# An H3 head and an S5 head on one core: row pairs of k, v, q and the output as two half transfers by parity, the filter's quarter matmuls for kv, and C's tiles transposed on TensorE

## The chip, the cores and the metric

The kernel runs on one core of one Trainium2 chip. The metric is the device time of one execution in microseconds, the median of several runs. All times here are of that core.

## The reference, cut to what matters

Two heads work side by side on sequences of S = 2048 steps and D = 1024 channels, and their outputs are put next to each other, bf16, [1, 2048, 2048]:

```python
def _A_ref(q, k, v, shift_k, ssm_k, ssm_D):
    for t in range(ks):                                   # ks = 4 taps
        k_shift = k_shift + k_pad[:, t:t + S, :] * shift_k[:, ks - 1 - t][None, None, :]
    kv = k_shift * v
    # a causal convolution over time, per channel, by transforms of length 2 * S = 4096
    y_f = rfft(pad(kv)) * rfft(pad(ssm_k))
    y = irfft(y_f)[:S] + kv * ssm_D
    return q * y
def _B_ref(x, Lambda_re, Lambda_im, B_re, B_im, C_re, C_im, log_dt, Dskip):
    Bu = jnp.einsum("bld,pd->blp", x, B_bar)              # B_bar, Lam_bar complex
    for t in range(L):
        h = Lam_bar[None, :] * h + Bu[:, t, :]
    return 2.0 * jnp.einsum("blp,dp->bld", hseq, Cmat).real + x * Dskip
return jnp.concatenate([a, b], axis=-1)
```

## The kernel before, in words

**Head B** goes through time in 16 chunks i of 128 steps. `x.i` loads a chunk transposed (a transposing DMA, L449). `U.i.jp.b` multiplies it by B, 16 matmuls of 128x128 (L468); `ue` copies the result from PSUM (ACT, L473). On DVE `r1` (L486), `r2` (L493) rotate it, `sc` scans (L499, two per chunk), `r3` (L486), `r4` (L505) rotate back; `cy` (ACT, L495) carries the last state over. `y.i.dh.part` (chunks 0 to 2, 14, 15; L515, L518) or `yq.i.k` (64x64 quarters of the array, chunks 3 to 13; L533) multiplies by C and adds the skip; `ye` evicts (L551). B is loaded in 16 tiles (`bl`), each transposed by 8 matmuls with the identity (`bT`, L417) and copied to BT (`bc`, ACT L433; one tile `bcv` on DVE, L431). Of C's 16 tiles eight come that way (`cl` L437, `cT` L417, `cc` ACT L441) and eight by a transposing DMA straight into CT (`cx`, L439). rtab, the scan's table of factors, is filled by ACT (`rta`, L379).

**Head A** does its transforms as matmuls. Time is split as t = 16 m + s: row m of 128 lies on partition m, and s = 0 to 15 counts steps. `kp.r` loads the row pair s = 2r, 2r + 1 of k (512 KB on 128 partitions) into a ring of 8 rows, `vp.r` of v, `qp.r` of q, all from SP's queue (L565 to L568, L573, L741). For each s `kvm`, `kva`, `kvb` (L582/584, L589, L595) make the 4-tap sum on DVE and `kvc` (L597) multiplies by v. `am.s.dh` (L602) is the first transform stage: two full 128x128 matmuls of 512 columns, one for each parity p of m, with F1t, whose rows of the other parity are zero. `ae` evicts (ACT, L608), `ast` stores to Ys_kv (POOL's queue, L611). The filter goes the same way in its own layout: `hl`, `hT` (transposes, L626), `hc` (ACT copy, L631), `hm` (L651), `he` (ACT, L659), `hst` (POOL's queue, L662). `hm` uses the quarter form: two row halves of the array by two column halves, FQt, four matmuls of 64x64 by 512 columns. The second stage works on 32 groups: `lw` loads the weights (L666, three slots), `lh`/`lk` the spectra (L671), `sh`/`sk` transform (quarters, L682), `she`/`ske` evict (L691, L698), `sw`/`swp` swap odd and even partitions by DMA (L702), `pr` multiplies (DVE, L708), `sa` transforms back (quarters, L720), `sae` evicts, `vst` stores Vs. The last stage: `vl` loads, `a3.s.dh` (L748) accumulates two full matmuls with Gt, one per parity, into one bank; `a3e` evicts, `qm` multiplies by q (DVE, L757), `ost`/`osp` store a row pair (POOL's or SP's queue, L758/759).

**What sets the order.** ORDER is a table of some 1500 words written into the kernel, run under a manual schedule: each task's instructions go to their engine's list in the table's order, and every engine runs its list in order. Letters after a colon give the slots: `a` a unit of the arena in SBUF (53 units of 2 KB per partition), `p` a PSUM bank of eight, `h` and `w` slots for states and weights. A task that reuses a slot waits for the slot's last reader. A suffix `v` puts an eviction on DVE. SP and POOL issue DMAs from their queues, each in order too, so a DMA behind one that waits is late as well.

Of the kernel before, what the change touches and what calls it, by code (L numbers as in the profile page):

```python
# [32 lines left out]
def a_constants():  # L33
# [37 lines left out]
bc.0.1 bc.7.0 bl.0.0:a46 tabA1:a24a51a14a12 kp.-1 bT.1.1:p2 x.0:a47 par_rest cl.0.0:a39 wb.1:p7 bT.5.0:p5 sin1
bl.3.0:a31 bcv.4.0 bT.0.0:p3 wbe.1 bT.4.1:p6 bc.1.1 tabA2 kring bl.3.1:a46 kvm.3:a26 gz bT.6.1:p1 bc.0.0 bl.1.0:a23
bc.4.1 U.0.2.0:a34p4 U.0.0.0:p2 sin2 bc.6.1 bl.2.1:a22 bT.3.1:p0 bc.5.0 x.1:a33 eo kvm.2:a18 kvm.1:a40 U.0.2.1
bT.1.0:p5 kva.2 cT.0.0:p1 bT.2.1:p3 bc.2.1 bT.3.0:p6 kva.1 kvb.2:a38 kva.3 bc.3.0 U.1.2.0:a36p7 stt U.1.2.1 bl.6.0:a50
bT.6.0:p3 kvb.1:a46 bl.7.1:a32 bc.3.1 U.0.1.0:p6 bT.7.1:p0 kp.-2 bc.1.0 bc.6.0 bc.7.1 U.0.1.1 U.0.0.1 ue.0.0 ue.0.1
vp.1:a48 cl.2.0:a22 z2 z1 cl.1.1:a31 cc.0.0 x.3:a21 cl.2.1:a44 ue.1.2 ue.0.2 U.0.3.0:p3 U.0.3.1 kvb.3:a32 ue.0.3
U.1.3.0:p6 U.1.0.0:p2 kvm.0:a13 cT.2.0:p0 U.1.3.1 U.1.1.0:p5 kvc.3 kvc.2 kva.0 r1.0:a48 cc.2.0 lw.1:w0 cl.1.0:a30
ue.1.3 cx.5.1 U.1.0.1 ue.1.0 cT.1.0:p3 cc.1.0 cl.3.0:a45 kvb.0:a39 am.2.1:p4p0 ae.2.1.1:a28 rta r2.0:h0 am.2.0:p6p2
cT.2.1:p1 cc.2.1 U.1.1.1 ue.1.1 cT.3.0:p3 vp.0:a42 kvc.1 U.3.2.0:a34p7 cc.3.0 ae.2.0.1 kvc.0 ae.2.0.0 kp.3 sc.0.1
U.3.2.1 hl.0.1:a24 cl.3.1:a20 cT.3.1:p0 sc.0.0 cc.3.1 am.3.0:p5p1 ae.3.1.0:a22 ae.2.1.0 r1.1:a42 hl.0.0 U.3.3.0:p3  # L80
U.3.3.1 cT.1.1:p0 cc.1.1 kp.2 hl.1.0:a48 cl.0.1:a38 ue.3.2 am.3.1:p4p1 ae.3.1.1 U.3.0.0:p6 ue.3.3 U.3.0.1 ue.3.0
ae.3.0.0 hl.1.1 am.1.1:p0p2 ae.1.1.1:a30 cx.5.0 am.0.0:p1p7 ae.0.1.0:a18 ae.3.0.1 r3.0:a12 hdv.1 ast.2 hdv.0 ast.3
U.3.1.0:p3 r4.0 ae.0.0.0 U.3.1.1 x.2:a52 cT.0.1:p5 am.1.0:p6p4 hT.0.4:p7 r2.1:h1 ae.1.0.1 am.0.1:p0p1 hT.0.7:p2
ae.1.1.0 hc.0.4:a16 hT.0.3:p4 ae.1.0.0 hT.0.0:p7 kvm.6:a12 ue.3.1 hT.0.6:p6 hc.0.3:a17 ae.0.0.1 cy.1 cc.0.1 ld_Q
hc.0.0:a46 ae.0.1.1 U.2.1.0:a44p3 r1.3:a40 U.2.1.1 ast.1 sc.1.1 U.2.2.0:p4 hc.0.7:a23 U.2.2.1 U.2.0.0:p5 ast.0 lw.0:w1
cx.6.0 cx.6.1 ue.2.2 U.2.0.1 cx.4.1 ue.2.1 hc.0.6:a20 ue.2.0 r2.3:h2 hT.0.1:p3 hT.0.2:p7 hc.0.1:a22 sc.1.0
hm.0.6.1:p1p2 hm.0.6.0:p4p6 he.0.6.0.0:a34 U.2.3.0:p0 hT.0.5:p3 hc.0.2:a41 U.2.3.1 hm.0.3.0:p5p4 he.0.6.1.1 he.0.6.1.0
he.0.3.0.0:a42 cx.7.0 kvm.5:a36 he.0.6.0.1 y.0.0.0:p7 kva.6 hc.0.5:a40 hm.0.7.1:p1p5 hm.0.3.1:p2p6 he.0.3.1.1 y.0.0.1
kvm.4:a24 he.0.3.1.0 he.0.7.1.1:a30 y.0.0.2 he.0.3.0.1 cx.4.0 cx.7.1 ue.2.3 he.0.7.1.0 y.0.0.3 hm.0.4.0:p2p6
ye.0.0:a17 hm.0.5.1:p5p4 hm.0.5.0:p0p3 he.0.4.0.0:a48 hst.0.6.1 he.0.5.0.0:a18 hst.0.6.0 he.0.5.1.0 he.0.5.0.1  # L90
y.0.1.0:p1 y.0.1.1 kvb.6:a20 he.0.5.1.1 kva.4 hm.0.4.1:p2p7 hm.0.7.0:p5p0 he.0.4.0.1 he.0.7.0.0 he.0.7.0.1 y.0.1.2
y.0.1.3 he.0.4.1.0 r3.1:a12 he.0.4.1.1 kvb.4:a23 hm.0.2.1:p6p4 he.0.2.1.0:a34 hst.0.3.1 x.4:a32 ye.0.1 he.0.2.1.1 r4.1
hm.0.0.1:p5p0 he.0.0.1.1:a50 U.4.1.0:a24p2 U.4.1.1 hm.0.2.0:p7p6 hm.0.0.0:p3p4 kva.5 he.0.2.0.1 hst.0.3.0 he.0.2.0.0
r1.2:a12 he.0.0.1.0 he.0.0.0.1 y.1.0.0:p1 hst.0.5.0 y.1.0.1 hst.0.5.1 kvb.5:a16 ue.4.1 hm.0.1.1:p7p5 hst.0.4.1
hm.0.1.0:p0p6 he.0.1.1.1:a38 he.0.1.0.1 y.1.0.2 vp.2:a28 hst.0.4.0 he.0.1.0.0 y.1.0.3 kvc.4 r2.2:h0 cy.2 he.0.0.0.0
ye.1.0:a18 kvc.5 am.5.1:p5p6 am.5.0:p4p2 am.4.1:p0p1 y.1.1.0:p3 y.1.1.1 he.0.1.1.0 hst.0.0.0 ae.5.1.1:a36 ae.4.0.1:a28
ae.5.1.0 hst.0.0.1 kp.5 am.4.0:p7p6 y.1.1.2 ae.4.1.0 vp.3:a26 ae.5.0.1 y.1.1.3 hl.3.0:a40 ae.5.0.0 hl.3.1 hd.3
ae.4.0.0 kvm.7:a12 hst.0.1.0 hl.2.0:a44 sc.2.1 kvc.6 hl.2.1 hd.2 am.6.0:p4p2 kva.7 ae.6.0.0:a22 ae.4.1.1 ast.5 sc.2.0
U.4.3.0:p6 ye.1.1 ae.6.1.0 kvb.7:a19 U.4.3.1 r3.2:a48 ue.4.3 am.6.1:p0p5 hT.1.1:p4 ae.6.0.1 kp.4 hc.1.1:a33 hT.1.3:p3
hc.1.3:a16 hst.0.1.1 ae.6.1.1 U.4.2.0:p2 hT.1.7:p0 U.4.2.1 yst.1 hc.1.7:a20 ue.4.2 ast.4 hT.1.6:p7 hc.1.6:a38  # L100
kvm.8:a12 U.4.0.0:p4 kvc.7 U.4.0.1 ue.4.0 r4.2 hT.1.0:p6 kva.8 ast.6 hc.1.0:a39 am.7.1:p0p2 am.7.0:p7p1 ae.7.1.0:a28
hT.1.4:p3 yst.0 hst.0.7.0 hc.1.4:a18 hst.0.2.0 ae.7.1.1 kvm.9:a48 y.2.0.0:p4 x.6:a37 ae.7.0.0 hm.1.3.1:p5p6 kvb.8:a36
he.1.3.1.1:a26 y.2.0.1 he.1.3.1.0 y.2.0.2 ae.7.0.1 cy.3 hm.1.7.1:p7p1 hm.1.3.0:p6p5 he.1.7.1.0:a16 hm.1.7.0:p3p0
he.1.3.0.1 he.1.3.0.0 he.1.7.0.1 he.1.7.0.0 kva.9 y.2.0.3 ye.2.0:a19 sc.3.1 vp.4:a22 y.2.1.0:p7 hT.1.2:p2 sc.3.0
hm.1.4.1:p0p6 hm.1.4.0:p3p5 kvc.8 hT.1.5:p4 r3.3:a44 y.2.1.1 ast.7 kvb.9:a18 y.2.1.2 hst.0.7.1 hst.1.3.1 he.1.7.1.1
y.2.1.3 he.1.4.1.0:a12 he.1.4.1.1 hst.1.3.0 hc.1.5:a20 he.1.4.0.1 he.1.4.0.0 am.8.1:p5p6 r4.3 ye.2.1 hst.1.4.1
ae.8.1.1:a40 am.8.0:p0p4 U.6.1.0:a14p1 hc.1.2:a52 U.6.1.1 ae.8.1.0 x.5:a36 ae.8.0.0 hst.0.2.1 ue.6.1 r1.4:a48 ae.8.0.1
# [729 lines left out]
```

## Time and profile before

| what | value |
|---|---|
| runs | 348.75, 350.41, 353.82 us; median 350.41 |
| profiled execution | 348.44 us, span 346.5 us, clock 0.998 |
| DMA, queue of SP (q1) / of POOL (q0) | 63.7% / 27.8% of 16 engines' span |
| transposing loads | x 16, C 8 |
| DMA issues of k, v, q from SP | k 8 of 512 KB (and 4 for the rows before the start), v 8, q 8 |

The span is the time from the first to the last instruction in the trace; the execution's own time also has what lies around it. A row of a group has the line, engine, operation, tiles, shapes and count, then the busy time and the mean length of one instruction; matmuls overlap, so that mean is longer than the distance from one to the next, which is read from the chain of waits. A row of waits has the engine that waits and the line that it waits at, what released it, total us, times and the longest. A row of DMA issues has the count, the size and the median time from issue to landing.

### The profile page before, as it was taken

How to read it: one execution, taken by the hardware profiler on the slowest of the kernel's cores; microseconds unless marked ns; L12 is line 12 of the kernel's file. 1: busy time of each engine (PE TensorE's matmuls, PEld its weight loads, DVE VectorE, ACT ScalarE, POOL GpSimd, SP SyncE). 2: the span in 40 equal slices, each digit the busy share in tenths (PEclk: the TensorE clock that was granted, in tenths of full speed). 3: DMA queues.
4: the chain of work that ended last, by engine and by line, in shares of the span. 5: the costliest groups of instructions: out<-in, count | busy, mean ns of one | idle time of the engine just before them, and what ended most of it. 6: DMA issues, size and time to landing. Idle time of an engine off the chain costs nothing.

```text
span 346.5 us, 11774 instructions
## 1 busy us (share of the span) xinstructions
PE 328.0 (95%) x5086; PEld 237.5 (69%) x5105; DVE 325.2 (94%) x263; ACT 272.3 (79%) x520; POOL 69.3 (20%) x114
## 2 busy tenths in 40 slices
PE   5889899999999999999999999999699999999994
PEld 2678789654856777688957877775376789754442
DVE  3999799999999999999999999999799999999991
ACT  6999999998999884599668899899689893314741
POOL 5000002142343163121100222211021133000021
PEclk9999999999999999999999999999999999999999
DMA  6999999979979879997896689999998898998995
GB/s 214 340 292 261 354 271 275 254 264 307 334 248 248 281 245 301 281 241 277 303 343 205 226 313 344 262 353 330 276 289 297 312 334 287 295 391 270 340 405 205
DMA packets 62752, 101.09 MB, mean 292 GB/s; under 512 B 29422, under 2 KB 31742, under 8 KB 62700
## 3 DMA queue, kind: packets, MB, share of 16 engines
q1 hardware_dynamic: 52652, 65.81, 63.7%
q0 software_dynamic: 10048, 34.52, 27.8%
q8 instruction: 40, 0.66, 0.8%
q14 instruction: 12, 0.10, 0.1%
HBM read 52.08 MB, written 33.55 MB: 247 GB/s over the span
## 4 chain that ended last, share of the span: by engine, by line
PE 68%; ACT 17%; DVE 7%; DMA 4%; issue 2%; SPq 1%; DVEq 0%; ACTq 0%
PE bank L468 24%; PE bank L533 15%; PE bank L515 10%; PE bank L682 4%; PE bank L720 4%; ACT BT L433 4%; PE bank L748 3%; PE bank L602 3%; DVE gslot L499 3%; PE bank L651 2%; ACT arena L608 2%; DMA wslot<-a_c_W 2%; ACT CT L441 2%; DVE arena L486 2%; ACT arena L473 2%
## 5 line engine op out<-in xcount | busy, mean ns | idle before, releaser
L468 PEld LDWEIGHTS <-BT 128*128 128x128 bf16 x2048 | 116.2, 98 | 13.0 <-issue 8.2
L468 PE MATMUL bank<-arena,BT 128*128 128x128 bf16 x2048 | 122.6, 219 | 1.6 <-DMA arena<-in_B_x_dram 0.9
L533 PE MATMUL bank<-CT,gslot 64*64 64x512 bf16 x1408 | 87.6, 377 | 0.0
L499 DVE TENSOR_TENSOR_SCAN gslot<-rtab,gslot 128x1040 bf16<-128x1040 f32 x32 | 73.0, 2312 | 0.1
L533 PEld LDWEIGHTS <-gslot 64*64 64x64 bf16 x1408 | 43.4, 107 | 23.9 <-ACT arena L698 0.6
L473 ACT CAST arena<-bank 128x512 bf16<-128x512 f32 x63 | 38.8, 655 | 11.6 <-PE bank L468 11.6
L608 ACT CAST arena<-bank 128x512 bf16<-128x512 f32 x64 | 37.2, 670 | 5.8 <-PE bank L602 4.9
L515 PE MATMUL bank<-CT,gslot 128*128 128x512 bf16 x154 | 38.1, 380 | 0.6 <-issue 0.3
L691 ACT CAST arena<-bank 128x512 bf16<-128x512 f32 x59 | 32.5, 615 | 7.8 <-PE bank L682 7.2
L486 DVE TENSOR_TENSOR arena<-arena,Z 128x4096 bf16<-128x4096 bf16 x16 | 36.5, 2284 | 2.2 <-ACT arena L473 2.1
L708 DVE TENSOR_TENSOR arena<-arena 128x4096 bf16<-128x4096 bf16 x16 | 36.3, 2285 | 1.7 <-ACT gslot L495 0.8
L728 ACT CAST arena<-bank 128x512 bf16<-128x512 f32 x61 | 33.3, 630 | 5.4 <-PE bank L720 5.3
L486 DVE TENSOR_TENSOR arena<-gslot,Z 128x4096 bf16<-128x4096 bf16 x16 | 36.6, 2288 | 0.3
L698 ACT CAST arena<-bank 128x512 bf16<-128x512 f32 x61 | 34.2, 616 | 3.3 <-PE bank L682 2.8
L659 ACT CAST arena<-bank 128x512 bf16<-128x512 f32 x64 | 35.2, 689 | 1.0 <-PE bank L651 0.7
L551 ACT CAST arena<-bank 128x512 bf16<-128x512 f32 x29 | 17.7, 616 | 16.3 <-PE bank L533 8.7
L582 DVE TENSOR_TENSOR arena<-arena 128x4096 bf16<-128x4096 bf16 (+3 forms) x16 | 30.0, 1886 | 0.1
L662 POOL DMA_DIRECT2D Ys_h<-arena x32 | 22.9, 728 | 29.0 <-ACT arena L659 23.1
L611 POOL DMA_DIRECT2D Ys_kv<-arena x16 | 10.9, 688 | 87.1 <-ACT arena L608 71.8
L515 PEld LDWEIGHTS <-gslot 128*128 128x128 bf16 x160 | 14.0, 98 | 17.1 <-issue 2.6
L702 POOL DMA_DIRECT2D arena<-arena x20 | 10.7, 538 | 70.8 <-ACT arena L691 46.9
L682 PE MATMUL bank<-arena,wslot 64*64 64x512 bf16 x256 | 21.5, 381 | 3.0 <-DMA wslot<-a_c_W 3.0
(104 smaller groups left out, 427.7 us busy)
## 6 DMA issues: line engine op xcount, KB each, us to landing
Ys_kv<-arena POOLq DMA_DIRECT2D x16, 512.0 KB, 4.9
Ys_h<-arena POOLq DMA_DIRECT2D x32, 256.0 KB, 3.8
arena<-Ys_h SPq DMA_DIRECT2D x16, 512.0 KB, 5.3
arena<-Ys_kv SPq DMA_DIRECT2D x16, 512.0 KB, 6.4
Vs<-arena POOLq DMA_DIRECT2D x16, 512.0 KB, 5.8
arena<-Vs SPq DMA_DIRECT2D x16, 512.0 KB, 6.9
arena<-arena POOLq DMA_DIRECT2D x20, 256.0 KB, 4.1
arena<-in_A_k_dram SPq DMA_DIRECT2D x8, 512.0 KB, 6.0
```

What stands on the lines that cost most here:

```text
L468: nc.tensor.matmul(pu[:, w, jl, :], BT[:, 2 * jp + jl, w, d, :], xT[:, d, :], start=(d == 0), stop=(d == ND - 1))
L473: either("ue", lambda cp, i, jp: cp(st["u", i][:, :, 2 * jp:2 * jp + 2, :], st.pop(("pu", i, jp))))
L486: nc.vector.tensor_mul(m, s_, win(Z))
L499: nc.vector.tensor_tensor_scan(gf, rtab[:].rearrange("p j t -> p (j t)"), gf, 0.0, ALU.mult, ALU.add)
L515: nc.tensor.matmul(py, h[:, w, j, 2:GW], CT[:, j, w, dh * 512:(dh + 1) * 512], start=(j == 0 and w == 0), stop=False)
L533: mm = nc.tensor.matmul(st["py", i, dh][cols, cs(r)], lhs(dh, rows, c), rhs(dh, rows), start=first, stop=last)
L608: cp(st["ysb", n2][:, p, dh * 512:(dh + 1) * 512], st.pop(("pa", n2, p, dh)))
L659: cp(o, st.pop(("pb", hf, s, e, r)).rearrange("p (n c t) -> p n c t", n=2, c=2))
L682: nc.tensor.matmul(st["ps", nm, g, l][64 * dh:64 * dh + 64, :], st["w", i][rows, a * WC:a * WC + 64], st[nm, i][rows, a, dh * 512:(dh + 1) ...
L698: cp(st["x16", i][:, a, l, :], st.pop(("ps", "k", g, l)))
L708: nc.vector.tensor_mul(hab, st.pop(("x16", i)).rearrange("p a l d -> p (a l d)").unsqueeze(1).to_broadcast([P, 2, 2 * D]), hab)
L728: cp(st["vsb", i][:, a, dh * 512:(dh + 1) * 512], st.pop(("pv", g, dh)))
```

## The change

- k, v, q and head A's output are viewed as t = 32 n + 16 p + s: partition 64 p + n holds row n of parity p. Each load or store of a row pair becomes two transfers of 256 KB, one per parity, on 64 partitions each: tasks `kpa`/`kpb`, `vpa`/`vpb`, `qpa`/`qpb` (p = 0 and 1), from SP's queue, or POOL's with the suffix `g`; `ost` and `osp` issue two DMAs.
- `am` runs in quarters through a helper shared with `hm` (L615), four 64x64 matmuls with FQt. F1t and the load `ld_Q` are gone; `ld_F` loads FQt.
- `a3` (L759) is two matmuls with Gt of 64 columns, each of a parity into its own half of the bank's partitions, without accumulation.
- All 16 C tiles come by `cl`, `cT`, `cc`; `cx` is gone. rtab is filled by DVE (`rt`), and two B tiles are copied by DVE.
- ORDER is written anew from end to end, with other slots.

```diff
-    F1 = np.stack([tr * (m % 2 == p)[:, None] for p in range(2)], axis=1)
     FQ = np.concatenate([tr[::2], tr[::2]], axis=0)
-    G = np.stack([tr.T * (m % 2 == p)[None, :] * 2 / NFFT for p in range(2)], axis=1)
+    G = tr[::2].T * 2 / NFFT
...
-    kr, vr, qr, oar = (a.rearrange("(m s) d -> m s d", s=16) for a in (k, v, q, out_a))
+    kr, vr, qr, oar = (a.rearrange("(n p s) d -> n p s d", p=2, s=16) for a in (k, v, q, out_a))
...
+    def half(dma, t_, dr, r, p):
+        dma(t_[64 * p:64 * p + 64, :, :], dr[:, p, 2 * r:2 * r + 2, :])
+
+    def kp(dma, r, p):
         s0 = (2 * r + 4) % KR
         t_ = ring()[:, s0:s0 + 2, :]
         if r >= 0:
-            spd(t_, kr[:, 2 * r:2 * r + 2, :])
+            half(dma, t_, kr, r, p)
...
+    def row_pair(nm, dma, dr, r, p):
+        if (nm, r) not in st:
+            st[nm, r] = sb(2).rearrange("p (s d) -> p s d", s=2)
+        half(dma, st[nm, r], dr, r, p)
+
+    for p_, e_ in enumerate("ab"):
+        for q_, dma_ in (("", spd), ("g", gpd)):
+            E["kp" + e_ + q_] = lambda r, p=p_, dma=dma_: kp(dma, r, p)
...
+    def f1_quarters(outs, src):
+        for a in range(2):
+            for r in range(2):
+                rows, cols = slice(64 * r, 64 * r + 64), slice(64 * a, 64 * a + 64)
+                nc.tensor.matmul(outs[r][cols, :], FQt[rows, cols], src[rows], start=True, stop=True)
+
     def am(n2, dh):
+        outs = [bank(), bank()]
         for p in range(2):
-            st["pa", n2, p, dh] = bank()
-            nc.tensor.matmul(st["pa", n2, p, dh], F1t[:, p, :], st["kv", n2][:, dh * 512:(dh + 1) * 512], start=True, stop=True)
+            st["pa", n2, p, dh] = outs[p]
+        f1_quarters(outs, st["kv", n2][:, dh * 512:(dh + 1) * 512])
...
         for p in range(2):
-            nc.tensor.matmul(pt, Gt[:, p, :], st["vv", n2][:, p, dh * 512:(dh + 1) * 512], start=(p == 0), stop=(p == 1))
+            nc.tensor.matmul(pt[64 * p:64 * p + 64, :], Gt[:], st["vv", n2][:, p, dh * 512:(dh + 1) * 512], start=True, stop=True)
```

ACT's list just ahead of chunk 0's first y. Before, these rows lead up to the first filter eviction (L659; L631 copies the filter's transposes, L473 evicts U):

```order
L441 COPY CT<-bank_101 128x8x128
L631 COPY arena<-bank_103 128x1024
L608 CAST arena<-bank_97 128x512
L631 COPY arena<-bank_98 128x1024
L473 CAST arena<-bank_100 128x2x256
L473 CAST arena<-bank_99 128x2x256
L631 COPY arena<-bank_102 128x1024
L473 CAST arena<-bank_101 128x2x256
L631 COPY arena<-bank_99 128x1024
L659 CAST arena<-bank_100 128x4x128
```

Now the rows up to the one that frees the first y's bank (bank_95; L675 is the filter eviction, L627 am's):

```order
L675 CAST arena<-bank_96 128x4x128
L441 COPY CT<-bank_97 128x8x128
L473 CAST arena<-bank_98 128x2x256
L441 COPY CT<-bank_95 128x8x128
L473 CAST arena<-bank_101 128x2x256
L675 CAST arena<-bank_99 128x4x128
L441 COPY CT<-bank_96 128x8x128
L675 CAST arena<-bank_98 128x4x128
L473 CAST arena<-bank_97 128x2x256
L627 CAST arena<-bank_96 128x512
L675 CAST arena<-bank_95 128x4x128
```

Ahead of the last row stand 23 filter evictions and 13 C copies now; ahead of the last row of before none and 8.

PE around an `am`. Before, two of them between transposes, each matmul 128 columns of the array wide:

```order
L417 MATMUL bank_99<-ident,arena 128x128
L602 LDWEIGHTS F1t
L602 MATMUL bank_100<-arena,F1t 128x512
L602 LDWEIGHTS F1t
L602 MATMUL bank_96<-arena,F1t 128x512
L602 LDWEIGHTS F1t
L602 MATMUL bank_102<-arena,F1t 128x512
L602 LDWEIGHTS F1t
L602 MATMUL bank_98<-arena,F1t 128x512
L417 LDWEIGHTS arena
```

Now one of them between two U:

```order
L468 MATMUL bank_100<-arena,BT 128x128
L615 LDWEIGHTS FQt
L615 MATMUL bank_101<-arena,FQt 64x512
L615 LDWEIGHTS FQt
L615 MATMUL bank_99<-arena,FQt 64x512
L615 LDWEIGHTS FQt
L615 MATMUL bank_101<-arena,FQt 64x512
L615 LDWEIGHTS FQt
L615 MATMUL bank_99<-arena,FQt 64x512
L468 LDWEIGHTS BT
```

Both banks are written by four quarters instead of two full matmuls, and the array changes its shape ahead of and behind the group.

The load of v's rows 4 and 5. Before, SP's queue had it between plain and transposing loads:

```order
L449 DMA_TRANSPOSE arena<-in_B_x_dram 128x8x128
L573 DMA arena<-in_A_v_dram 128x2048
L565 DMA arena<-in_A_k_dram 128x2048
L573 DMA arena<-in_A_v_dram 128x2048
```

Now one half is on SP's queue and the other on POOL's, among the stores of the first stage (L630) and of the filter (L678):

```order
L630 DMA Ys_kv<-arena 256x1x1024 x3
L678 DMA Ys_h<-arena 128x2x512
L630 DMA Ys_kv<-arena 256x1x1024
L562 DMA arena<-in_A_v_dram 64x2048
L562 DMA arena<-in_A_k_dram 64x2048
L678 DMA Ys_h<-arena 128x2x512 x9
```

On DVE the tile comes free with the first of these rows (kvb of row 4) and is read by the last (kvc of row 4):

```order
L607 TENSOR_TENSOR arena<-arena 128x1024
L601 TENSOR_TENSOR arena<-arena 128x2048
L486 TENSOR_TENSOR arena<-arena,Z_77 128x4096
L607 TENSOR_TENSOR arena<-arena 128x1024
L493 TENSOR_TENSOR gslot_88<-arena 128x16x128
L609 TENSOR_TENSOR arena<-arena 128x1024
```

More of the change, by code (lines that the diff above doesn't have):

```diff
@@ L71 @@
[L71 to L80, printed above, removed]
@@ L91 @@
[L91 to L95, printed above, removed]
@@ L188 @@
+ysg.15.0 y.15.1.3 ye.15.1 ysh.15.1
 """
```

277 lines of the change are left out of this document (144 added, 133 removed).

## The prediction, made before the result was known

> **What bounds the kernel now.** I read the page's busy shares and its chain first, then the chain of waits stretch by stretch, the busy time by stretch, the list of waits and the DMA issues.
>
> ```profile
> PE 328.0 (95%) x5086; PEld 237.5 (69%) x5105; DVE 325.2 (94%) x263; ACT 272.3 (79%) x520; POOL 69.3 (20%) x114
> PE 68%; ACT 17%; DVE 7%; DMA 4%; issue 2%; SPq 1%; DVEq 0%; ACTq 0%
> ```
>
> Two engines are nearly full, and the chain that ended last has a third in it: ACT. The busy time by stretch (columns PE, PEld, DVE, ACT, POOL, clock, DMA share, GB/s) says where each holds:
>
> ```profile
> 24.00:32.00 8.00, 7.12 (x125) 6.88 (x123) 8.00 (x22) 8.00 (x15) 0.00 (x0) 1.00 1.10 298
> 40.00:60.00 20.00, 19.82 (x310) 18.46 (x313) 20.00 (x17) 20.00 (x34) 2.86 (x5) 1.00 1.03 274
> 80.00:120.00 40.00, 39.84 (x479) 26.83 (x480) 40.00 (x29) 37.50 (x74) 13.72 (x20) 1.00 0.89 282
> 240.00:260.00 20.00, 16.91 (x318) 11.83 (x307) 17.32 (x12) 15.52 (x33) 2.35 (x4) 1.00 1.05 287
> ```
>
> Up to 60 us ACT and DVE are full and the DMA engines saturated (share above 1); later PE and DVE are full and ACT is not. The chain changes hands at 61 us (start, length, what):
>
> ```profile
> 59.47 0.91 ACT arena L631
> 60.38 0.98 ACT arena L473 x2
> 61.36 0.04 issue
> 61.41 1.14 PE bank L626 x16
> 65.83 0.32 PE bank L515
> ```
>
> Until 61.36 the chain is ACT's list of evictions and copies, and ACT is full. Then PE leads, and L515 at 65.83 is chunk 0's first y. From there PE runs to the end with one real stall:
>
> ```profile
> 243.68 7.34 DMA wslot<-a_c_W
> 332.69 1.22 DVE L505 TENSOR_TENSOR gslot<-arena 128x2048 bf16<-128x2048 bf16 x1
> 342.05 0.07 PE bank L518
> 342.15 0.58 ACT arena L551
> ```
>
> PE ends at 342.12; eviction and store take it to 346.5, a tail of 4.4. The chain counts PE's side, but the last r4 on DVE (L505, 332.69 to 333.9) releases y of chunk 15 at 335: DVE is never more than a microsecond or two behind. The waits by engine:
>
> ```profile
> POOL Ys_h L662 <- ACT arena L659: 23.1, 10, 7.8
> PE bank L682 <- DMA wslot<-a_c_W: 3.0, 1, 3.0
> DVE arena L691 <- PE bank L682: 2.5, 2, 2.3
> DVE arena L486 <- ACT arena L473: 2.1, 1, 2.1
> ```
>
> The W load that took 7.34 cost PE 3.0 and DVE 2.3. Its like takes (median, last column) 4.0:
>
> ```profile
> wslot<-a_c_W SPq DMA_DIRECT2D x16, 160.0 KB, 4.0
> ```
>
> **The change part by part.** All sums are against the profiled execution: 348.44 us, span 346.5, so 1.94 outside the span. The runs' median, 350.41, is 2.0 above it.
>
> *When PE takes over.* What ACT has in its list ahead of y's gate sets this. Unit costs on ACT:
>
> ```profile
> 35.72 0.90 ACT CT L441
> 50.34 3.41 ACT arena L608 x7
> L379 ACT COPY rtab<-r 128x1024 f32<-128x1024 f32 x1 | 1.2, 1239 | 0.0
> ```
>
> A C copy is 0.90, like L631 above, a cast 3.41/7 = 0.49. Before, the list up to the piece that ends at 61.36 holds 8 C copies, 16 casts of am, 4 copies of hT, 15 of B and rtab's. Now the first y's bank is freed by the 24th filter eviction (the order of ACT in the section on the change), and ahead of it and with it stand 13 C copies, 13 casts of am, 8 copies of hT, 14 of B and 24 filter casts; the ue casts are 14 in both. So: 24 x 0.49 = +11.8, 4 x 0.91 = +3.6, 5 x 0.90 = +4.5, -3 x 0.49 = -1.5, one B copy -0.9, rtab -1.0; together +16.5. ACT reaches the gate at 61.36 + 16.5 = 77.9 and y starts at about 78.0, 12.2 later. The bounds: were the longer list not in the way at all, y would start at the 65.8 of before; were PE's own work ahead of y (below) not hidden under it, somewhat later than 78. I take 78.0, since ACT is full in both stretches above and its rows don't depend on the load.
>
> *PE after the first y.* Unit costs:
>
> ```profile
> 99.43 0.34 PE bank L651 x4
> 102.62 0.97 PE bank L515 x4
> 105.07 0.56 PE bank L651 x8
> 329.84 0.86 PE bank L515 x4
> 83.00 1.29 PE bank L602 x6
> 331.68 1.29 PE bank L748 x6
> 88.84 1.79 PE bank L468 x32
> ```
>
> A full 512-column matmul takes 1.29/6 = 0.215, alike in L602 and L748. L651 is the quarter form that am now gets: four cost 0.34 behind a full matmul and a further four 0.56 - 0.34 = 0.22, so the array's change of shape costs 0.12; back to full it costs 0.97 - 0.86 = 0.11. I use 0.115 a change. U's 16 matmuls are 0.895, a transpose 1.14/16 = 0.07, and 8 of them about 0.5.
>
> Counted from the order of PE, behind the first y: am, 24 at 0.43 become 22 at 0.22, 10.3 - 4.8 = -5.5. a3, 64 full matmuls at 0.215 = 13.8 become 32 pairs of 64-column ones. No row shows such a pair: at best it runs side by side like the quarters (0.215 a pair, -6.9), at worst one after the other (0). I take -6.9, nearest to L651, where two column halves run at once. Four more U tasks, which ACT's list has pushed behind the first y, +3.6; ten fewer hm, -2.2; one C task, +0.5; changes of shape 60 to 73, +1.5. Sum -9.0. The other C transposes (7 more tasks) and 25 more changes lie ahead of the first y, under ACT's 78 us, and cost nothing unless ACT gets there sooner; then they are 3.5 + 2.9.
>
> Before, PE had 342.12 - 65.83 = 276.3. Now 267.3. The W loads keep a lead like before's (in the order of PE the shortest has 3.7 us of work between the slot's last reader and the first use, before 4.1, against a median landing of 4.0), and whether one is hit again is chance; I take off half of the 3.0, 265.8. So 78.0 + 265.8 = 343.8, and with the tail 4.4 the span is 348.2.
>
> *DVE.* It gains rtab's fill (as on ACT 1.2 for 1024 fp32 columns) and a second B copy, 0.68:
>
> ```profile
> L431 DVE COPY BT<-bank 128x1024 bf16<-128x1024 bf16 x1 | 0.7, 683 | 0.0
> ```
>
> +1.9 in all, less the 2.3 of L691 that hung on W. ACT's longer list also feeds DVE: summed in the same way, the ue casts of chunks 1 and 3 are done about 1 us after DVE asks for them at r1, 0 to 2 in all, much like the 2.1 at chunk 0 (L486) that is in the sum already; I take 0. So r4 of chunk 15 ends at 333.9 - 0.4 = 333.5, plus what the new loads cost, and from its end to the span's end it was 12.6: 346.1. PE's 348.2 stands 2.1 above, so DVE decides only from 2.1 us of new waits on.
>
> *The half transfers, and C's loads.*
>
> ```profile
> arena<-in_A_k_dram SPq DMA_DIRECT2D x8, 512.0 KB, 6.0
> arena<-in_A_v_dram SPq DMA_DIRECT2D x8, 512.0 KB, 6.8
> arena<-arena POOLq DMA_DIRECT2D x20, 256.0 KB, 4.1
> Ys_h<-arena POOLq DMA_DIRECT2D x32, 256.0 KB, 3.8
> CT<-in_B_C_re_dram SPq DMA_TRANSPOSE x4, 5.6
> ```
>
> The swaps (L702) already touch 64 partitions with 256 KB and land in 4.1; the filter stores, 128 partitions with 256 KB, in 3.8. On that a half costs what half a transfer costs, so nothing; and the eight transposing loads that go, like the eight plain ones that come, land under ACT's list. The bound is that a half takes as long as a whole: v's 6.8 twice. Where it is tight is v of rows 4 and 5: its tile comes free at the fourth kvb (L607 now), and four DVE instructions later (L601, L486, L607, L493, some 5 us by their like in the order of DVE) L609 needs it. A landing of 4 to 7 costs DVE 0 to 2. The second half stands on POOL's queue behind filter stores that wait for ACT, as L662 did for up to 7.8; behind it there wait a k half and the next filter stores, which nobody needs soon, and for the half itself waits L609, and with it all of DVE. Together 0 to 10. The store ahead of that half has its casts listed some ten us before, so I take the low end, 2, which the 2.1 in hand covers: nothing in the sum. Of the other 19 halves of k and v ahead of the first y only one is listed next to its use, a k half of rows 6 and 7; it stands on SP's queue, which runs ahead of the table, as before's v of rows 4 and 5 did, and I count nothing for it. The halves of q are asked for long after they land.
>
> The page "SBUF — State Buffer" of the Trainium skill, "Can I just issue two DMAs to hit both halves?", says that two such transfers serialize and reach only half the ports each (196 against 328 GB/s at 1 MiB). By the row of the swaps the sum gains nothing; by the page a half would take nearly the time of a whole, and the sum would be that of the late halves below. No row here has a transfer of one contiguous half.
>
> **Sum**: span 348.2, execution 350.1; at the 2.0 by which the median stood above the profiled execution it would be 352, at the 0.3 of the fastest run shown (348.75) 350.4. I take the lower of the two, 350.5: no change.
>
> **The rivals.**
>
> *Stalls go, PE sets everything (346).* Without W's 1.5 and the 2.2 of small gaps that 276.3 holds over its unit costs, the span is about 344.5, the execution 346.5. For: the transposing loads that saturate the start go. Against: W's 7.34 came at 243 us, where no C load was before either. To beat 2% (343.4) ACT's gate would also have to fall by 3, say by C copies that no longer wait for loads; but ACT was full from 24 to 32 and from 40 to 60, and cannot have waited there.
>
> *The halves arrive late (358).* Place: v and k halves in the first 90 us, where the DMA share is above 1. Mechanism: each half holds the DMA engines as long as a whole did, 256 KB more at the 298 GB/s of 24 to 32 us, 0.9 us for each of the 20 ahead of the first y, some 18 us of transfer where there is no room; what POOL sends comes last, behind the store's wait of up to 7.8, and L609 stands still for it. It decides from the 2.1 that DVE has in hand: 7.8 + 2 - 2.1 is +7.7, an execution of 358. For: POOL's stores wait for ACT in before already, 23.1 in all. Against: the swaps' 4.1.
>
> *PE's saving is not there (357).* Pairs that run one after the other give +6.9, a span of 355, an execution of 357. For: no such pair in the trace. Against: L651's four quarters in 0.22.
>
> *The change doesn't do what it says*: the casts on ACT, not the C loads, fill the first 78 us, so taking away transposing loads shows in no time at all. That is in my sum already.
>
> **How the numbers follow.** Forecast 0.60; stalls go 0.18, of which 0.08 beat 2%; late halves 0.13; no saving 0.09. A measurement of this kernel, whose runs lie 5 us apart, tells about 2% (343.4 to 357.4) from no change. Faster 0.08; slower 0.20 (0.17 of the last two, which lie at that edge, and 0.03 of the forecast's own upper end); same 0.72. The range reaches from 344.5 to 358.5: below it a part of the second case is left out, above it a part of the third, where ACT's delay and a late half add up.
>
> **What would show it.** Right: L515's first start near 78, with ACT full ahead of it; L615 in quarters of 0.22; twelve L759 matmuls in about 1.3 instead of 12 x 0.215; PE idle in the first 78 us up by about 8; PE and DVE within 3 of each other at the end. Wrong: waits of DVE at L609 or L596 on DMA over 2 us; pairs of L759 at 0.43; y's start before 72 or after 82; k and v halves that land later than the 6.0 and 6.8 of the wholes.

## The result, and the profile after

The changed kernel took 374.46 us (median of four executions: 368.60, 371.55, 377.37, 378.21), the kernel before 349.58 beside it: a ratio of 1.0625 with a 95% interval of 1.0548 to 1.0702. It is slower by 21 to 25 us, far above the forecast 350.5 and above the range's end of 358.5. Of each kernel some executions are quicker and some slower (those more than 1.5% above its quickest), and differences between kernels are taken below between the means of the quicker ones; here that is 21. The profiled execution is the longest of the four (378.21, span 376.4, granted clock 0.978 against 0.998), so its rows are read for where the time goes and in what order, and sizes are taken from the runs below.

The page's busy line and its chain by engine, answering to the two lines shown first of before:

```profile
PE 335.3 (89%) x5225; PEld 240.2 (64%) x5233; DVE 328.4 (87%) x266; ACT 278.5 (74%) x526; POOL 82.7 (22%) x137
PE 56%; DMA 21%; ACT 16%; issue 3%; SPq 2%; POOL 0%; DVE 0%; ACTq 0%; POOLq 0%; DVEq 0%
```

No engine is full any more, and transfers hold 21% of the chain, where they held 4%. The transfers of 7 us and more in the chain, and two pieces of the last stage's matmuls (start, length, what):

```profile
4.28 10.51 DMA arena<-in_B_B_im_dram
88.16 9.40 DMA Ys_kv<-arena
137.76 11.86 DMA Ys_h<-arena
273.71 12.22 DMA Vs<-arena
293.41 7.34 DMA arena<-Ys_h
328.95 1.00 PE bank L759 x8
333.00 16.65 DMA arena<-Vs
360.03 1.63 PE bank L759 x14
```

The largest, 16.65 us, is a Vs load of the last stage; Vs loads are whole transfers that the change did not touch. Their neighbours there are the halves of q (task, number, KB each, median us from issue to landing):

```profile
arena<-Vs SPq DMA_DIRECT2D x16, 512.0 KB, 8.6
arena<-in_A_q_dram SPq DMA_DIRECT2D x9, 256.0 KB, 8.9
arena<-in_A_v_dram SPq DMA_DIRECT2D x8, 256.0 KB, 7.0
arena<-in_A_k_dram POOLq DMA_DIRECT2D x10, 256.0 KB, 7.1
arena<-in_A_k_dram SPq DMA_DIRECT2D x7, 256.0 KB, 5.8
```

A half of 256 KB lands about as late as a whole of 512 KB did: k at 5.8 and 7.1 beside 6.0, v at 7.0 beside 6.8, q at 8.9 beside 4.8. The busy time by stretch (columns as in the prediction), the first four of before and then of after, and the last but one of after:

```profile
0.00:20.00 20.00, 13.89 (x121) 9.43 (x121) 14.17 (x36) 16.57 (x24) 5.01 (x16) 1.00 0.89 290
20.00:40.00 20.00, 17.28 (x283) 16.08 (x284) 17.91 (x28) 20.00 (x37) 0.00 (x0) 1.00 1.13 296
40.00:60.00 20.00, 19.82 (x310) 18.46 (x313) 20.00 (x17) 20.00 (x34) 2.86 (x5) 1.00 1.03 274
60.00:80.00 20.00, 19.51 (x213) 11.67 (x213) 20.00 (x17) 19.74 (x38) 6.15 (x9) 1.00 0.91 257
```

```profile
0.00:20.00 20.00, 9.56 (x58) 5.98 (x59) 12.86 (x36) 12.50 (x19) 7.51 (x20) 1.00 0.91 234
20.00:40.00 20.00, 14.76 (x149) 13.64 (x150) 17.01 (x28) 19.26 (x33) 1.55 (x3) 0.91 1.09 292
40.00:60.00 20.00, 18.42 (x280) 15.29 (x278) 16.49 (x18) 19.91 (x33) 3.17 (x5) 1.00 1.00 250
60.00:80.00 20.00, 19.51 (x323) 17.00 (x322) 19.70 (x17) 20.00 (x36) 9.60 (x14) 1.00 0.88 255
...
340.00:360.00 20.00, 15.21 (x143) 7.04 (x141) 15.39 (x12) 7.59 (x16) 1.47 (x3) 0.91 1.03 281
```

So the time goes at two ends. In the first 80 us PE is busy 62.3 instead of 70.5, and ACT, which the sum had as full, 71.7 instead of 76.3. In the last stage (340 to 360) PE and DVE stand idle a quarter of the time while the DMA share is 1.03. The y matmuls divide the span there; their rows say when the first and the last starts, of before and of after:

```profile
L515 PE MATMUL bank<-CT,gslot x154: 379/379/391, 65.8 to 341.7; 128*128 128x512 bf16 x154
```

```profile
L515 PE MATMUL bank<-CT,gslot x152: 376/379/608, 83.6 to 368.7; 128*128 128x512 bf16 x152
```

The start moved by 17.8 (forecast 12.2), and the rest behind it went from 275.9 to 285.1, up by 9.2 where it was to fall by 10.5.

### The profile page after: what moved, and what is told of

Its sections match the earlier page's. It is cut to its first block, busy times and chain, and to the rows that moved or that the text cites. A ratio compares the mean times of both kernels' runs of the same rounds, so it can differ in the third digit from the quotient of the medians.

```text
span 376.4 us, 12108 instructions
## 1 busy us (share of the span) xinstructions
PE 335.3 (89%) x5225; PEld 240.2 (64%) x5233; DVE 328.4 (87%) x266; ACT 278.5 (74%) x526; POOL 82.7 (22%) x137
## 4 chain that ended last, share of the span: by engine, by line
PE 56%; DMA 21%; ACT 16%; issue 3%; SPq 2%; POOL 0%; DVE 0%; ACTq 0%; POOLq 0%; DVEq 0%
PE bank L468 23%; PE bank L533 13%; PE bank L515 7%; DMA arena<-Vs 4%; PE bank L736 4%; PE bank L698 3%; DMA Vs<-arena 3%; ACT CT L441 3%; DMA Ys_h<-arena 3%; ACT arena L627 3%; DMA arena<-in_B_B_im_dram 3%; DMA wslot<-a_c_W 3%; DMA Ys_kv<-arena 2%; PE bank L615 2%; ACT arena L675 2%
## 5 line engine op out<-in xcount | busy, mean ns | idle before, releaser
L468 PE MATMUL bank<-arena,BT 128*128 128x128 bf16 x2048 | 124.0, 221 | 6.1 <-ACT BT L433 2.1
L533 PE MATMUL bank<-CT,gslot 64*64 64x512 bf16 x1408 | 89.2, 380 | 0.0
L533 PEld LDWEIGHTS <-gslot 64*64 64x64 bf16 x1408 | 41.2, 108 | 27.5 <-issue 1.6
L473 ACT CAST arena<-bank 128x512 bf16<-128x512 f32 x64 | 39.9, 662 | 15.9 <-PE bank L468 15.1
L627 ACT CAST arena<-bank 128x512 bf16<-128x512 f32 x60 | 33.1, 629 | 10.8 <-DMA Ys_h<-arena 5.5
L707 ACT CAST arena<-bank 128x512 bf16<-128x512 f32 x59 | 32.4, 627 | 10.4 <-PE bank L698 6.0
L675 ACT CAST arena<-bank 128x512 bf16<-128x512 f32 x64 | 38.4, 742 | 2.2 <-PE bank L615 1.7
L744 ACT CAST arena<-bank 128x512 bf16<-128x512 f32 x61 | 32.8, 628 | 6.4 <-PE bank L736 6.3
L714 ACT CAST arena<-bank 128x512 bf16<-128x512 f32 x57 | 31.3, 615 | 7.8 <-PE bank L698 7.8
L417 PE MATMUL bank<-ident,arena 128*128 128x128 bf16 x256 | 25.5, 275 | 12.7 <-DMA arena<-in_B_B_re_dram 4.4
L594 DVE TENSOR_TENSOR arena<-arena 128x4096 bf16<-128x4096 bf16 (+3 forms) x16 | 30.1, 1884 | 3.1 <-DMA arena<-in_A_k_dram 3.0
L417 PEld LDWEIGHTS <-arena 128*128 128x128 bf16 x256 | 22.0, 126 | 16.3 <-DMA arena<-in_B_B_im_dram 5.2
L678 POOL DMA_DIRECT2D Ys_h<-arena x32 | 23.7, 742 | 26.1 <-ACT arena L675 18.7
L551 ACT CAST arena<-bank 128x512 bf16<-128x512 f32 x31 | 18.6, 627 | 13.5 <-PE bank L518 11.2
L766 ACT CAST arena<-bank 128x512 bf16<-128x512 f32 x30 | 16.1, 605 | 11.7 <-PE bank L759 11.6
```

The lines of the kernel that those rows point to most:

```text
L417: nc.tensor.transpose(pt[:, d, :], src[:, d * P:(d + 1) * P], ident[:])
L468: nc.tensor.matmul(pu[:, w, jl, :], BT[:, 2 * jp + jl, w, d, :], xT[:, d, :], start=(d == 0), stop=(d == ND - 1))
L473: either("ue", lambda cp, i, jp: cp(st["u", i][:, :, 2 * jp:2 * jp + 2, :], st.pop(("pu", i, jp))))
L533: mm = nc.tensor.matmul(st["py", i, dh][cols, cs(r)], lhs(dh, rows, c), rhs(dh, rows), start=first, stop=last)
L627: cp(st["ysb", n2][:, p, dh * 512:(dh + 1) * 512], st.pop(("pa", n2, p, dh)))
L675: cp(o, st.pop(("pb", hf, s, e, r)).rearrange("p (n c t) -> p n c t", n=2, c=2))
```

## The experiments

The theory formed on these rows: transfers that fill or empty 64 neighbouring partitions are slow and slow what runs beside them; that costs more than half of the loss, the rest is the new order. The rivals: it is the number of transfers; it is the stride in DRAM; it is the new order alone. Every run was timed against the kernel before on the same chip (its medians there 348.7 to 351.6). Landings (us, median, of SP's queue where POOL's carries some too) are from each profiled execution. "4 KB" is the mean time of a packet of 4 KB on SP's queue, taken over the trace's packet records; it is a mean of all such packets on the queue, not of the halves' alone, and in b_rows, whose split loads have packets of 2 KB, it leaves these out. "over before" is the difference defined above, in us, with the number of the kernel's executions that it rests on.

| kernel | median us | over before | ratio [95%] | q lands | Vs lands | 4 KB ns |
|---|---|---|---|---|---|---|
| before | 349.6 | 0 | 1 | 4.8 | 6.9 | 185 |
| changed | 374.5 | 21.3 (2) | 1.0625 [1.0548, 1.0702] | 8.9 | 8.6 | 213 |
| b_half64 | 363.3 | 14.1 (4) | 1.0416 [1.0342, 1.0491] | 10.3 | 10.8 | 238 |
| b_half32 | 366.0 | 15.6 (3) | 1.0521 [1.0418, 1.0624] | 10.5 | 10.2 | 235 |
| b_oddeven | 369.1 | 18.9 (3) | 1.0556 [1.0459, 1.0652] | 6.7 | 7.9 | 183 |
| b_rows | 354.6 | -0.5 (1) | none | 6.5 | 7.8 | 189 |
| b_half_q | 362.8 | 6.4 (1) | none | 10.1 | 10.5 | 201 |
| b_half_kv | 355.7 | 3.6 (3) | 1.0113 [1.0022, 1.0204] | 5.0 | 6.1 | 220 |
| b_math | 349.6 | -3.1 (2) | none | 4.5 | 6.7 | 181 |
| b_layout | 365.6 | 16.1 (3) | 1.0453 [1.0397, 1.0509] | 9.3 | 8.3 | 236 |
| b_one | 627.8 | 276 (4) | 1.7875 [1.7694, 1.8057] | 17 in its chain | 17 in its chain | 188 |
| a_whole | 360.8 | 8.3 (2) | 1.0251 [1.0176, 1.0325] | 6.7 | 7.3 | 188 |
| a_half_kv | 363.5 | 9.2 (2) | 1.0272 [1.0133, 1.0410] | 6.6 | 5.5 | 198 |
| a_whole_cx | 366.2 | 13.9 (3) | 1.0406 [1.0307, 1.0505] | 6.4 | 7.0 | 188 |
| a_order | 372.7 | 19.4 (2) | none | 6.3 | 5.3 | 189 |

Where no ratio stands, none is on record with an interval, and the difference is the weaker for it.

**Four ways of halving, in the order of before.** Order and arithmetic are those of before; each load of k, v and q and each store of a row pair becomes two of 256 KB:

```
+    def two(dma, dst, src, store=False):
+        for p in range(2):
+            a, b = slice(64 * p, 64 * p + 64), slice(p, P, 2)               # b_half64
+            a, b = slice(64 * p, 64 * p + 64), slice(64 * p, 64 * p + 64)   # b_half32
+            a, b = slice(p, P, 2), slice(p, P, 2)                           # b_oddeven
+            a = b = (slice(None), slice(p, p + 1))                          # b_rows
+            dma(src[b], dst[a]) if store else dma(dst[a], src[b])
-            spd(t_, kr[:, 2 * r:2 * r + 2, :])
+            two(spd, t_, kr[:, 2 * r:2 * r + 2, :])
```

(and so for v, q and the output).

> The kernel before, with each whole load and store of a row pair of k, v, q and the output split in two as the change splits them (64 neighbouring partitions each, every second row in memory), same queue, same place. Rows of head A land on the wrong partitions, so head A's output is not the reference's. Theory 1 (the halves themselves slow the DMA engines down: a half takes as long as a whole and what runs beside it gets slower): 6 us or more slower than before, the landings of k and v halves at 6 to 7 us, and 4 KB packets longer on average. Theory 2 (the halves are harmless; the new table of the order is late by itself, by ACT's longer list and by loads behind waiting stores): within 2 us of before.

> The kernel before, with the same transfers split in two by neighbouring partitions, 0 to 63 and 64 to 127, and neighbouring rows in memory; the output is the reference's. Theory 1: as slow as with every second row, 6 us or more over before, since the partitions make it. If only the distance of the rows in memory matters: like before, while the split with every second row is slow. Theory 2: within 2 us of before.

> The kernel before, with the same transfers split in two by odd and even partitions: as many transfers of the same size and packets, 64 partitions each, but spread over all 128. Theory 1 in its narrow form (neighbouring partitions share their way into SBUF): within 2 us of before. If the number of transfers alone makes it: as slow as the split in neighbouring halves. Theory 2: within 2 us of before.

> The kernel before, with each row pair of k, v, q and the output moved as two transfers of 256 KB that each cover all 128 partitions (one of the pair's two rows each, 2 KB a partition); the output is the reference's. It has as many transfers as the split in halves, without narrowing them. Theory A (the number of transfers makes the loss: SP's queue has eight in flight and then goes at the pace of their landings, so half the bytes are under way): 360 us or more, as with the halves. Theory B (64 partitions make it: packets into half the partitions are slower): 354 us or less.

The two that use 64 neighbouring partitions cost 14 and 16 us, with every second row of DRAM or with rows side by side: the stride in DRAM is not it. The same number of transfers of the same size over all 128 partitions (b_rows) costs nothing in its quickest execution (348.3) and some 6 in the three others (near 354.7; before had one of 354.2 beside it). The number is not it either, or a small part. The landings of b_half64, beside those of before:

```profile
arena<-Vs SPq DMA_DIRECT2D x16, 512.0 KB, 10.8
arena<-in_A_k_dram SPq DMA_DIRECT2D x16, 256.0 KB, 6.5
arena<-in_A_v_dram SPq DMA_DIRECT2D x16, 256.0 KB, 4.7
arena<-in_A_q_dram SPq DMA_DIRECT2D x16, 256.0 KB, 10.3
```

```profile
arena<-Vs SPq DMA_DIRECT2D x16, 512.0 KB, 6.9
arena<-in_A_q_dram SPq DMA_DIRECT2D x8, 512.0 KB, 4.8
```

Half the bytes take twice as long for q (10.3 instead of 4.8) and as long as the whole for k (6.5 beside 6.0); only v's halves land sooner (4.7 beside 6.8). The untouched Vs loads beside q take 10.8 instead of 6.9. The bytes moved on the queue are the same, yet its packets hold the sixteen engines 68.9% of the span (363.9 us) instead of 63.7% (346.5): 30 us more of sixteen engines' time, which are full in much of the span.

The version with odd and even partitions contradicts its expected time and must be read by stretch. Its packets are as fast as before's (183 ns), and its last stage is as full as before's; its loss comes at 20 to 40 and 100 to 120 us, where the DMA engines have little to do:

```profile
20.00:40.00 20.00, 16.69 (x247) 16.35 (x244) 19.54 (x28) 16.17 (x31) 0.00 (x0) 0.83 0.42 134
...
100.00:120.00 20.00, 13.46 (x137) 11.12 (x136) 11.59 (x9) 11.47 (x18) 3.93 (x6) 0.83 0.64 190
...
320.00:340.00 20.00, 19.80 (x359) 10.70 (x359) 19.79 (x13) 5.03 (x11) 0.00 (x0) 1.00 0.94 335
340.00:360.00 20.00, 19.89 (x100) 9.40 (x101) 19.84 (x18) 12.32 (x26) 4.79 (x8) 1.00 0.97 353
```

There SP's queue waits 14.3 us, up to 36, before it issues halves of v and 11.2, up to 101, before halves of k (waits of the queue at L567: total, times, longest), for instructions on which no load of k or v waits in before:

```profile
SPq L567 <- PE bank L634: 14.8, 2, 11.2
SPq L567 <- DVE Z L357: 14.3, 1, 14.3
```

So this run does not price the halves; that the waits were added for the strided partitions is likely, but was not tried apart. What it does show: halves over 64 partitions that are not neighbours leave the last stage full.

**Which halves.** b_half_q puts only q and the output into b_half64's halves, b_half_kv only k and v:

```
-        spd(st["qt", r], qr[:, 2 * r:2 * r + 2, :])
+        two(spd, st["qt", r], qr[:, 2 * r:2 * r + 2, :])
-    E["osp"] = lambda r: spd(oar[:, 2 * r:2 * r + 2, :], st["ot", r])
+    E["osp"] = lambda r: two(spd, st["ot", r], oar[:, 2 * r:2 * r + 2, :], True)
```

> The kernel before with only q and the output split in neighbouring halves, k and v whole; rows of q's product land on the wrong partitions, so head A's output is not the reference's. If the loss of the split falls late, where q's loads meet those of the last stage: 357 us or more, most of the 13 us. If it falls early, at k and v: within 3 us of before.

> The kernel before with only k and v in half transfers of 64 neighbouring partitions (even rows to 0-63, odd to 64-127), q and the output whole; the arithmetic is unchanged, so head A's rows are mixed wrongly. Theory (the halves cost in the last stage, where q, output and Vs share the queues; in the first two stages k and v are asked for early enough): 349 to 354 us, that is at most 4 us more. Rival (halves cost wherever they are, by their number): half of the 13.5 us of the version with all in halves or more, 356 us and up.

q and the output cost 6.4 in the shortest execution (355.15, the one profiled; the three others took 361.2 to 364.9), between the two figures expected; k and v cost 3.6, at the upper edge of what was expected for them. Together that is 10, less than the 14 of b_half64, so the two do not simply add. In b_half_q the first y starts at 66.1 as before, and the two stretches that were 19.80 and 19.89 in before lose 4.3 of PE, at a DMA share of 1.04 and 1.03:

```profile
300.00:320.00 20.00, 17.34 (x300) 8.53 (x293) 18.49 (x14) 3.09 (x6) 0.55 (x1) 1.00 1.04 281
320.00:340.00 20.00, 18.07 (x89) 8.06 (x88) 15.87 (x13) 12.33 (x25) 4.20 (x7) 1.00 1.03 318
```

What waits there is the last stage's matmul for Vs and DVE's product for q:

```profile
PE bank L756 <- DMA arena<-Vs: 3.5, 3, 1.7
```

```profile
DVE arena L765 <- DMA arena<-in_A_q_dram: 2.9, 1, 2.9
```

**The halves taken out of the changed kernel.** a_whole sends each row pair whole at the place of its first half (k's rows before the start stay in parts); a_half_kv does so for q and the output only:

```
+    seen = set()
     def half(dma, t_, dr, r, p):
-        dma(t_[64 * p:64 * p + 64, :, :], dr[:, p, 2 * r:2 * r + 2, :])
+        if (id(dr), r) not in seen:
+            seen.add((id(dr), r))
+            dma(t_, whole[id(dr)][:, 2 * r:2 * r + 2, :])
```

> The changed kernel, with one whole transfer on 128 partitions at the place of the first half of each pair and none at the second, the same for the output's stores; rows of head A land on the wrong partitions, so head A's output is not the reference's. Theory 1: the loss is mostly gone, 349 to 355 us. Theory 2: 363 us or more, like the change.

> The changed kernel with q and the output back in whole transfers (at the first half's place), k and v still in halves; head A's rows of q and of the output then do not fit the layout. Theory: q's and the output's halves are most of what halves cost, so it stands within 4 us of the changed kernel with all whole (360.8), 358 to 366 us. Rival (with k and v on the path from the start in the new order, their halves cost most): 368 us or more, near the changed kernel's 374.

The loss of 21.3 falls to 9.2 without q's and the output's halves, as expected, and to 8.3 without any: 12.1 and 0.9, 13 in all, near before's order (14). a_whole, at 360.8, lies between its two theories: 8 us are left that the halves do not explain. Its y row:

```profile
L516 PE MATMUL bank<-CT,gslot x152: 377/379/391, 80.5 to 357.1; 128*128 128x512 bf16 x152
```

Its first y is 14.7 later than before's, and its rest, 276.6, is no shorter than the 275.9 of before, although am and a3 cost less (the row is from its execution of 363.7).

**The arithmetic alone, and with the layout, in the order of before.** b_math has am in quarters and a3 in half-width pairs on whole transfers in the old row order (head A's transform thus mixes the wrong rows); b_layout has the same arithmetic with the changed layout in halves.

```
-            nc.tensor.matmul(st["pa", n2, p, dh], F1t[:, p, :], ...)
+        for a in range(2):
+            for r in range(2):
+                rows, cols = slice(64 * r, 64 * r + 64), slice(64 * a, 64 * a + 64)
+                nc.tensor.matmul(st["pa", n2, r, dh][cols, :], FQt[rows, cols], ...)
-            nc.tensor.matmul(pt, Gt[:, p, :], ..., start=(p == 0), stop=(p == 1))
+            nc.tensor.matmul(pt[64 * p:64 * p + 64, :], Gt[:], ..., start=True, stop=True)
```

> The kernel before in its own order, with am in quarters and the last stage in half-width pairs, and whole transfers in the old layout, so head A's output is not the reference's. By the sum of the prediction PE loses 6.8 for am and 6.9 for the pairs and gains 55 changes of shape at 0.115, 7.4 less in all, of which DVE lets about 5 through: 343 to 348 us. If the saving on PE is not there or buys nothing: 349 us or more.

> The kernel before in its own order with the whole of head A's new layout: halves by parity on the queues of before, am in quarters, pairs in the last stage; C and the rest as before; the output is the reference's. If the halves cost 13 and the quarters give 5: 355 to 361 us. If the change's loss is its halves alone: about 370. If the new order made it: 350 or less.

b_math gains 3 us in its two shorter executions (344.9 and 346.3, inside the expected 343 to 348); the two others took 352.9 and 353.7, so its median is 349.6 and the gain is not certain. The sum had 7.4 less work on PE. In the profiled execution of 344.9 PE and DVE are both at 95%, and y on PE waits for DVE's rotation back (r4, L501 here):

```profile
PE 325.3 (95%) x5169; PEld 232.2 (68%) x5169; DVE 325.0 (95%) x263; ACT 272.6 (79%) x520; POOL 69.0 (20%) x113
```

```profile
PE bank L511 <- DVE gslot L501: 2.7, 2, 1.5
```

With the layout in halves added it is 365.6, between the expected 355 to 361 and 370: 16 over before and 19 over b_math, so on top of the cheaper matmuls the halves cost somewhat more than on before.

**One transfer for both halves.** b_one keeps b_layout but describes each row pair as one transfer over all 128 partitions, the parity as the outermost of the DRAM side's dimensions:

```
+        v = bass.AP(src.tensor, src.offset, [[row, 2], [2 * row, 64], [1, 2 * D]])
+        dma(dst, v)
```

> The kernel before with the changed layout (even rows on partitions 0-63, odd rows on 64-127), the quarters and the half-width pairs, but every row pair of k, v, q and of the output as ONE transfer that fills all 128 partitions, its DRAM side written as parity, row, 2048 elements. Nothing is left out. Theory (the loss in this order is that of transfers that end on 64 neighbouring partitions, not of the layout, the stride in DRAM or the quarters and pairs): it behaves as the version with quarters, pairs and whole transfers did, 345 to 351 us, q lands in 4.5 to 5.5 us and the Vs loads in 6.5 to 7.5. Rival (the every-second-row order of DRAM, or a transfer whose outermost dimension is 2, is what is slow): over 358 us and q at 8 us or more.

The rival held, and far more than it said. A transfer described so takes 17 to 26 us, though a 4 KB packet takes 188 ns as ever:

```profile
262.55 26.42 DMA arena<-in_A_v_dram
470.23 16.97 DMA arena<-in_A_q_dram
```

Two of the sixteen engines are at work on it at a time. From 593 to 603 us the store of an output row pair, issued at 591.6, runs alone, all its packets 4 KB, and the DMA share (last but one) is 0.13, 2 of 16:

```profile
593.00:603.00 10.00, 0.00 (x0) 0.00 (x0) 0.00 (x0) 0.00 (x0) 0.00 (x0) 0.50 0.13 46
```

That it is one engine for each step of the outermost dimension fits the two, but no run has another number of steps. The run computes something other than the reference, so "Nothing is left out" was wrong, and it is read for these times alone. It gives no mended version.

**What is left: the order, C, the matmuls.** a_whole_cx is a_whole with six C tiles (d = 5 to 7) loaded transposing again; a_order is the changed kernel's order, queues and C loads with the layout, the matmuls and the whole transfers of before:

```
-cl.5.1:a35 ... cT.5.1:p2 ... cc.5.1      # a_whole_cx: six such triples
+cx.5.1
```

> The changed kernel with whole transfers (360.8) and with six of its sixteen C tiles (d = 5, 6, 7) back as transposing loads, so that six C copies leave ScalarE's list ahead of the first y and six transposes TensorE's; head A's rows do not fit the layout. Theory (what is left of the loss is the later y, and C's copies are part of what makes it late): y starts about 3.6 us earlier than 80.5 and the time falls to 354-359 us. Rival (the remaining loss is the second stage's waits on DMA round trips and the order itself): y may start earlier but the time stays within 2 us of 360.8; or the transposing loads hold the queue up and it gets slower.

> The order, the queues and the C loads of the changed kernel, with the layout, the matmuls (padded F1, accumulating a3) and the whole transfers of the kernel before; nothing is left out. It differs from the changed kernel with whole transfers (360.8, ratio 1.025) by the matmuls alone. Theory (the new order alone costs about 11 us, its first y is late and its waits on DMA fill what the cheaper matmuls leave free): 359 to 366 us, first y near 81. Rival (the cheaper matmuls are worth their 10 us in this order, the order costs 20): 368 to 375 us.

a_whole_cx lost another 5.6 us instead of gaining, and its first y did not come 3.6 earlier:

```profile
L516 PE MATMUL bank<-CT,gslot x152: 376/379/634, 82.1 to 362.2; 128*128 128x512 bf16 x152
```

Only three of the six copies stood ahead of the first y (10 C copies run before it here, 13 in a_whole), and with them gone ACT is no longer full from 60 to 80 us (18.46 of 20, in a_whole 20.00). The chain then runs to ACT's filter eviction (L680) over the landing of a filter store:

```profile
72.43 8.92 DMA Ys_h<-arena
```

So taking C copies out of ACT's list does not by itself bring y forward, and loading C plainly shows as no part of the loss; whether the transposing loads or something behind them cost the 5.6 was not tried apart. In a_order, with nothing of the change but the order, C's loads and the fills and copies that moved to DVE, the first y is as late as in the changed kernel:

```profile
L521 PE MATMUL bank<-CT,gslot x153: 379/379/390, 83.3 to 365.0; 128*128 128x512 bf16 x153
```

It takes 372.7 (shortest 367.4 and 371.3; before 351.1 beside it). The theory that went with it (359 to 366) fell, the rival (368 to 375) held: the order with C costs 19, and the cheaper matmuls win back 11 of it in a_whole. That they win 11 here and 3 in b_math fits that DVE has 11% of a_order's span free, while in before's order PE and DVE are full together; it was not tried apart.

Put together, over before: 19 (order, with C) - 11 (matmuls) + 13 (halves) = 21. The parts depend on the order in which they are added. The other way round, in before's order first, they are -3 (matmuls, b_math) + 19 (halves, b_layout) + 5 (from b_layout to the changed kernel, the new order with C) = 21. So the halves cost 13 to 19 whichever way; the new order costs 19 by itself, but only 5 where the halves already hold the kernel up.

## Why the prediction was wrong

- **"On that a half costs what half a transfer costs, so nothing."** This step failed, and with it the forecast: halves cost 13 to 19 us, where the sum had nothing. The row of the swaps (256 KB in 4.1) was the wrong neighbour: a swap reads and writes odd and even partitions, spread over all 128, and b_oddeven showed that with such packets the queue's mean stays at 183 ns, while with 64 neighbours it is 235 to 238. The page "SBUF — State Buffer" of the Trainium skill, section "Can I just issue two DMAs to hit both halves?", says that two such transfers serialize and that only one transfer over all 128 partitions reaches all the ports. The runs agree in the size, with k's half at 6.5 against the whole's 6.0 and q's at 10.3 against 4.8, though v's half took 4.7 against 6.8; the serializing itself no run shows. The prediction quoted the rule and went by the row.
- **The rival "the halves arrive late (358)"** had the mechanism, the wrong place and too small a price: it looked at k and v in the first 90 us; they cost 1 to 4. "The halves of q are asked for long after they land" left out that they share the queues with the Vs loads and the stores: q and the output cost 6 to 12, in a stage that had no room before. The row of before for that stretch, which the prediction does not show, has the DMA share at 1.01:

```profile
320.00:340.00 20.00, 19.89 (x101) 9.44 (x102) 19.36 (x16) 10.67 (x22) 2.99 (x5) 1.00 1.01 375
```

What happened to the Vs loads beside them (from 6.9 to 8.6 in the changed kernel, to 10.8 in b_half64) had no term at all.
- **"y starts at about 78.0."** 83.6. The halves are not needed for it: a_order, with whole transfers and in an execution of 371.3, has 83.3, and a_whole 80.5. The casts and copies counted ahead of y were right, to one; the step that failed is "and ACT is full". In the first 80 us it is 4.6 less busy than before, 4.1 of that in the first 20, and y is 5.6 later than forecast; in a_order it is 4.0 less busy and y 5.3 later, in a_whole 1.6 and 2.5. The first transfer in the chain above is a B load of 10.51 us from 4.28 on; that such loads keep ACT waiting is read from these rows and was not tried apart. In a_whole_cx three C copies fewer ahead of y did not make it earlier.
- **"PE after the first y 265.8."** The unit costs were right. Eight half-width matmuls took 1.00 and fourteen 1.63, so six more took 0.63, and a pair costs 0.21, the 0.215 that was taken; four quarters took 0.34 and eight 0.56, as counted:

```profile
112.87 0.56 PE bank L615 x8
70.97 0.34 PE bank L615 x4
```

  The step that failed is that nothing else would grow behind the first y. By the y rows the rest is 281.7 in a_order, 276.6 in a_whole, 285.1 in the changed kernel: +5.8 from the order, -5.1 from the matmuls (a_whole's y is also 2.8 earlier than a_order's), +8.5 from the halves. The rows are of executions of 371.3, 363.7 and 378.2 us, the last two above their kernels' medians, so the three differences are rough. In a_order's chain stand a Vs store and a spectra load of the second stage, where before had a swap of 5.29 and W's 7.34; that they make up the order's 5.8 was not tried apart, so the cause of the order's own cost stays open:

```profile
273.10 9.82 DMA Vs<-arena
288.70 8.48 DMA arena<-Ys_h
```

- **DVE "decides only from 2.1 us of new waits on."** Its waits at L609 for v and at L594, the first of the tap products, for k, 3.2 and 3.0, were over the 2 us named as a sign, and the largest is the last stage's:

```profile
DVE arena L768 <- ACT arena L766: 6.3, 2, 3.5
DVE arena L609 <- DMA arena<-in_A_v_dram: 3.2, 3, 2.2
DVE arena L594 <- DMA arena<-in_A_k_dram: 3.0, 1, 3.0
```

- **"PE's saving is not there"** and **"stalls go"** did not come about: the saving is there, and the stalls grew.

## What to carry to other kernels

Price a split transfer by a row with the same set of partitions, not by one with the same number of bytes, and then ask what else uses the queues in that stretch: here an untouched load beside it lost 3.9 us, and the split one 5.5. Where PE and DVE are both at 94%, cheaper matmuls bought 3 us of the 7.4 that they took off PE by the sum, so an order that is given up for them must be as good as the old one by itself; here the order alone, with C's loads, cost 19 us, which one run of the new order with the old arithmetic showed. Measure a part at both ends, though: added last, the same order cost 5. Of the versions run only b_math is quicker than the kernel before, by 3 us in two of its four executions, and it has the rows in the wrong layout.

## What the runs showed of the hardware

- Packets of 4 KB on SP's queue took 235 to 238 ns in the mean when k, v, q and the output moved in halves of 64 neighbouring partitions, against 185 with whole transfers and 183 with halves of every second partition; where only q's and the output's or only k's and v's transfers were halved, the mean was 201 and 220.
- A transfer whose outermost dimension had two steps took 17 to 26 us for 512 KB, against 4.8 to 6.8 for the whole with 128 rows, at an ordinary time per packet (188 ns); alone under way it kept 2 of the 16 engines busy (share 0.13).
- The granted clock was 0.83 in the two stretches of b_oddeven in which TensorE was busy for 16.69 and 13.46 of 20 us, and 0.79 over all of b_one; it was 1.00 in the changed kernel's first 20 us, with 9.56 busy.
